# Strassen groups that accumulate on copies in PSUM: linear attention followed by a SiLU MLP

## The chip, the cores and the metric

The kernel runs on one core of one Trainium2 chip. The metric is the device time of one execution in microseconds (us). The engines are named as in the profile: PE is TensorE (matrix products), PEld its weight loads, DVE is VectorE, ACT is ScalarE, POOL is GpSimd, SP is SyncE (here it only issues DMAs). PSUM, where PE writes, has 8 banks of 128 partitions x 512 fp32 values.

## The reference

```python
# q, k, v: (batch 8, heads 8, seq 576, dim 64) fp32; w_in: 512 x 2048; w_out: 2048 x 512
q_s = exp(q - max(q, -1)); q_s = q_s / (sum(q_s, -1) + 1e-09)      # softmax over dim
k_s = exp(k - max(k, 2));  k_s = k_s / (sum(k_s, 2) + 1e-09)       # softmax over seq
kv = einsum('bhsd,bhse->bhde', k_s, v)
x = einsum('bhsd,bhde->bhse', q_s, kv)                             # (8, 8, 576, 64)
x = x.transpose(0, 2, 1, 3).reshape(4608, 512)
h = x @ w_in
out = (h * (1 / (1 + exp(-h)))) @ w_out                            # fp32, 4608 x 512
```

## The kernel before

All work runs in one pass over the 4608 tokens. The attention part goes batch by batch (576 tokens), the two products of the MLP chunk by chunk. Chunk 0 is the 576 tokens of batch 0, chunk 1 the 448 tokens up to token 1024, chunks 2 to 8 have 512 tokens each.

**Attention, batch b.** The loads `lq`, `lk`, `lv` come in two halves `c` of four heads each. ACT takes exp (`eq`, `ek`). DVE sums q's rows and inverts the sums (`z`). POOL scales q (`n`) and casts v to bf16 (`vc`). q is turned over by PE and copied out (`tr`, `tc`, batches 0 and 1) or by a DMA on SP's queue (`tq`). PE forms k^T v (`kv`), DVE scales it (`kc`). PE forms x^T (`X`), and ACT or DVE copies it to SBUF as fp16 (`x`). The trailing letter a or v of an operation says ACT or DVE. Batches 0 and 3 to 7 are loaded through SP's queue, batches 1 and 2 and all weights (`W1...`, `W2...`, converted to fp16 on the way) through POOL's.

**First product and SiLU.** Chunk 0 is done plainly, 16 blocks of 128 rows of h (`w`; tanh `h`; DVE `v`), and its second product too (`p`, in PSUM banks 2 to 5). Half of chunk 1 is plain (`m` in banks 0 to 3, with SiLU `mu`). The other half of chunk 1, and chunks 2 to 8 whole, use Strassen's algorithm in Winograd's form: per chunk two groups g (1 and then 0), each with seven half-size products P1 to P7 (`g{t}.{g}.{i}`, 8 matmuls of 256 columns each), with sums of weights `WS` made once and differences of x (`xs`) per chunk. Each product fills a pair of banks. P1, P6, P7 and P4 add up in banks 0 and 1. P2, P5 and P3 go to a second pair, which `other` names: 6 and 7 for group 1, 2 and 3 for group 0. The four output blocks are:

- U11 = P1 + P2
- U12 = P1 + P6 + P5 + P3
- U21 = P1 + P6 + P7 + P4
- U22 = P1 + P6 + P7 + P5

Before, bank 0's pair is copied to SBUF after P1, after P6 and after P7 (`s{t}.{g}.0`, `.1`, `.2`; `group_snap`, L398 to L400). DVE then adds the second pair to each copy (`a...`; `group_add`, L402 to L405), and ACT takes the SiLU of the three sums from SBUF and of bank 0 straight from PSUM (`u...`; `group_silu`, L407 to L409). The next product may go into a pair only when the copy or sum that reads it is done.

**Second product.** For chunks 1 to 8 it is Strassen as well: products `b{t}.{i}.{m}` (8 matmuls of 256 columns each, banks 4 and 5, L503), sums `S`, `T` and `sa`, `sb`, `sc`, `wa`, `wb`, `wc`, `wl`, and stores `o` on SP's queue. The last chunk's are named `e`, with stores spread over three queues (`q...`).

**Order.** The program issues operations by name from the string `ORDER`, from left to right; each goes to the end of its engine's queue, and an engine works its queue in that order. Waits between engines follow from the data. Before, chunk 0's start (loads, transposes, first x^T) is written out ahead of `ORDER`. The sums over SBUF operands on DVE are `S`, `T`, `WS` and `xs`.

Of the kernel before, what the change touches and what calls it, by code (L numbers as in the profile page):

```python
# [22 lines left out]
    vc1.1a vc1.1b gcopy WS1.3 kv1 lv2.1 tc1.1b p8 tc1.1a kc1 WS0.3 xt1.0 xt1.1 x1.0a x1.1v p9 x1.2a x1.3v  # L23
    g1.1.1 xs1.1 xs1.2 xs1.4 g1.1.2 s1.1.0a WS0.4 p10 xs1.3 eq2.0 a1.1.0 p11 eq2.1 z2.0 g1.1.6 g1.1.5
    s1.1.1a z2.1 n2.0 p12 ek2.0 g1.1.7 p13 s1.1.2v n2.1 ek2.1 p14 a1.1.2 g1.1.4 p15 tq2 u1.1.4 g1.1.3 po2v
    vc2.1 po1a m0 po3v po0a a1.1.1 u1.1.0 vc2.0 m1 lk3.0 mu0 m2 T2 lq3.0 mu1 lq3.1 m3 u1.1.2 lk3.1 T3 m4
    lv3.0 u1.1.1 lv3.1 m5 T4 mu2 os0 mu4 kv2 mu5 m6 mu3 kc2 X2.0 mu6 X2.1 x2.0v m7 x2.1a x2.3a x2.2v g2.1.1
    mu7 xs2.1 xs2.2 g2.1.2 s2.1.0v b1.1.0 ek3.0 S1.1 g2.1.6 eq3.1 lk4.0 S1.2 b1.2.0 os1 s2.1.1a b1.1.1 xs2.3
    xs2.4 eq3.0 a2.1.0 g2.1.7 vc3.0 sa1 b1.2.1 lq4.0 z3.1 s2.1.2a g2.1.5 vc3.1 ek3.1 b1.6.0 a2.1.2 n3.1
    lk4.1 g2.1.4 z3.0 g2.1.3 u2.1.0 g2.0.2 u2.1.4 wa1 n3.0 b1.6.1 a2.1.1 u2.1.2 g2.0.1 sb1 S1.3 kv3 tq3  # L30
    s2.0.0a b1.5.0 kc3 u2.1.1 S1.4 g2.0.6 b1.7.0 s2.0.1v lv4.0 ek4.1 b1.7.1 lv4.1 a2.0.0 os3 g2.0.7 sc1
    ek4.0 b1.5.1 s2.0.2v g2.0.5 eq4.0 lk5.0 wc1 lq4.1 g2.0.4 a2.0.2 os2 b1.4.0 vc4.0 lk5.1 z4.0 u2.0.4
    g2.0.3 u2.0.2 b1.3.0 lv5.0 vc4.1 a2.0.1 u2.0.0 lq5.0 b1.4.1 n4.0 X3.0 wl1v X3.1 kv4 x3.0a x3.1v x3.2a
    b1.3.1 kc4 x3.3a xs3.1 u2.0.1 g3.1.1 xs3.2 wb1 g3.1.2 s3.1.0a xs3.3 xs3.4 g3.0.2 S2.1 g3.1.6 S2.2 eq4.1
    b2.2.0 s3.1.1a b2.1.0 z4.1 ek5.0 b2.1.1 a3.1.0 g3.1.7 n4.1 sa2 ek5.1 b2.6.0 s3.1.2v g3.1.5 vc5.0 tq4
    g3.1.4 a3.1.2 u3.1.0 b2.6.1 u3.1.4 S2.3 g3.1.3 sb2 lq5.1 g3.0.1 u3.1.2 a3.1.1 lv5.1 lk6.0 b2.7.0 s3.0.0a
    o1.0 S2.4 b2.2.1 u3.1.1 a3.0.0 g3.0.6 lv6.0 b2.7.1 s3.0.1v eq5.0 g3.0.5 wa2 g3.0.7 sc2 lq6.0 z5.0 b2.4.0
    s3.0.2a lk6.1 b2.5.0 vc5.1 eq5.1 a3.0.2 g3.0.4 o1.1 n5.0 z5.1 g3.0.3 u3.0.4 b2.5.1 a3.0.1 n5.1 u3.0.0
    b2.4.1 wc2 u3.0.2 X4.0 X4.1 kv5 x4.1v x4.0a tq5 wl2v b2.3.0 u3.0.1 x4.3v g4.1.1 xs4.1 x4.2a b2.3.1 xs4.2
    s4.1.0a S3.1 g4.1.2 wb2 g4.1.6 lq6.1 a4.1.0 ek6.1 b3.1.0 xs4.3 s4.1.1a b3.1.1 xs4.4 S3.2 ek6.0 g4.1.5  # L40
    g4.1.7 sa3 eq6.0 b3.2.0 s4.1.2v eq6.1 b3.2.1 lq7.0 kc5 lk7.0 b3.6.0 a4.1.2 lv6.1 lq7.1 g4.1.4 o2.0 wa3
    g4.1.3 z6.0 u4.1.4 b3.5.0 u4.1.0 S3.3 g4.0.1 lk7.1 b3.6.1 a4.1.1 s4.0.0a g4.0.2 sb3 u4.1.1 g4.0.6 a4.0.0
    b3.5.1 s4.0.1a S3.4 b3.7.0 vc6.1 u4.1.2 g4.0.7 z6.1 vc6.0 g4.0.5 s4.0.2a b3.7.1 a4.0.2 n6.1 g4.0.4 sc3
    u4.0.2 g4.0.3 wc3 n6.0 b3.3.0 u4.0.4 a4.0.1 b3.4.0 u4.0.0 X5.0 X5.1 kv6 x5.0a x5.1v tq6 x5.3a x5.2v
    b3.3.1 u4.0.1 xs5.1 g5.1.1 xs5.2 wb3 b3.4.1 s5.1.0v o2.1 ek7.1 g5.1.2 kc6 g5.1.6 wl3a xs5.3 xs5.4 a5.1.0
# [25 lines left out]
def kernel(  # L71
# [9 lines left out]
    nc = tc.nc  # L81
# [196 lines left out]
    def xt_mm(b, cc, col, n, bank, dst):  # L278
        for r in range(2):
            for s in range(2):  # L280
                h = slice(s * 64, (s + 1) * 64)
                nc.tensor.matmul(  # L282
                    out=PS[r * 64:(r + 1) * 64, bank + s, dst:dst + n],
                    lhsT=kvn[b % 3][h, cc, r, :],
                    rhs=st[b]["qT"][h, col // P:(col + n) // P, cc, r * 64:(r + 1) * 64],
                )
# [7 lines left out]
    def x_mm(t, cc):  # L294
        for b, col, n, dst in pieces(t):
            xt_mm(b, cc, col, n, XBANK[2 * cc], dst)
# [114 lines left out]
    def group(t, g, i):  # L411
        bank = 0 if i in (1, 6, 7, 4) else other(t, g)
# [10 lines left out]
        for p in range(4):  # L423
            for c in range(2):
                nc.tensor.matmul(  # L425
                    out=PS[:, bank + p // 2, (p % 2) * HT:(p % 2) * HT + width(t)],
                    lhsT=a[:, c, p * 128:(p + 1) * 128],
                    rhs=bb[:, c, 0:width(t)],
                    start=(i in (1, 2, 5) and c == 0 and p % 2 == 0),
                    stop=(i in (2, 3, 4) and c == 1 and p % 2 == 1),  # L430
                    skip_group_check=True,
                )


# [404 lines left out]
```

## Time and profile before

| | |
|---|---|
| runs (3) | 257.86 us median, 256.9 to 258.57 |
| the profiled execution | 258.61 us |
| its span, first to last instruction | 256.6 us |
| PE, PEld busy | 249.1 us (97%), 204.2 us (80%) |
| DVE, ACT, POOL busy | 206.2 us (80%), 190.9 us (74%), 65.8 us (26%) |
| granted PE clock | 1.00 |
| HBM read, written | 36.70 MB, 9.44 MB |
| chain that ended last, largest parts | PE 76%, DMA 11%, issue 5% |

"Busy" is the time in which an engine has an instruction in work. The chain that ended last is followed back from the last instruction: at each step to what released it. A line with two names joined by `<-` reads output from input, with buffer numbers left out. In the groups by shape, the numbers behind the bar are the total busy time, the mean of one instruction in ns, and the engine's idle time just ahead of it with what ended that.

### The profile page before, as it was taken

The page shows a single profiled execution, that of the slowest core. Times are in us where ns is not written, and L with a number is a line of the kernel's source. Part 1 is how long each engine was busy: PE and PEld are TensorE (multiplying, and loading weights), DVE is VectorE, ACT ScalarE, POOL GpSimd, SP SyncE. Part 2 cuts the span into 40 slices and gives each one's busy share as a digit, 9 for nine tenths or more (in the row PEclk, how much of TensorE's full clock was granted, in tenths as well). Part 3 has the DMA queues.
Part 4 walks back from the last instruction along what each step waited for, and adds up shares of the span by engine and source line. Part 5 has one row for each costly group of instructions (what it writes and reads, how often), then busy time and mean ns, then how long its engine had stood idle before and what let it go on. Part 6 is the DMA issues. An engine that isn't in the chain of part 4 may idle for free.

```text
span 256.6 us, 6459 instructions
## 1 busy us (share of the span) xinstructions
PE 249.1 (97%) x2732; PEld 204.2 (80%) x2732; DVE 206.2 (80%) x276; ACT 190.9 (74%) x225; POOL 65.8 (26%) x62
## 2 busy tenths in 40 slices
PE   8799999999999999999999999999999999999994
PEld 3457746656888888888888888888888888888883
DVE  2958999888999898998987986896579836886752
ACT  5766876699999999999879988737587665664411
POOL 1753593650450622350073030006000000000022
PEclk9999999999999999999999999999999999999999
DMA  7999999979959957996874960021807000600365
GB/s 248 348 181 297 302 301 283 351 140 393 378 128 213 403 187 137 361 335 168 276 266 68 224 236 3 3 52 32 163 14 153 13 0 4 148 18 0 66 141 123
DMA packets 36044, 45.89 MB, mean 179 GB/s; under 512 B 16288, under 2 KB 21088, under 8 KB 36016
## 3 DMA queue, kind: packets, MB, share of 16 engines
q1 hardware_dynamic: 29456, 33.56, 45.5%
q0 software_dynamic: 6160, 11.60, 17.8%
q10 hardware_dynamic: 400, 0.33, 0.6%
q8 instruction: 21, 0.34, 0.5%
q14 instruction: 7, 0.06, 0.1%
HBM read 36.70 MB, written 9.44 MB: 180 GB/s over the span
## 4 chain that ended last, share of the span: by engine, by line
PE 76%; DMA 11%; issue 5%; POOL 3%; ACT 2%; DVE 1%; ACTq 0%; POOLq 0%
PE PS L503 37%; PE PS L425 33%; DMA qt<-in_q_dram 5%; DMA kt<-in_k_dram 5%; PE PS L335 3%; PE PS L248 2%; PE PS L282 2%; POOL W L564 1%; DMA out_dram<-ow 1%; POOL qt L152 1%; DVE GT L323 1%; ACT L409 0%; POOL W L570 0%; ACT sg L320 0%; ACT GT L409 0%
## 5 line engine op out<-in xcount | busy, mean ns | idle before, releaser
L403 DVE TENSOR_TENSOR h<-PS,h 128x1024 f32<-128x1024 f32 (+1 forms) x45 | 54.2, 1206 | 9.3 <-PE PS L425 7.8
L503 PEld LDWEIGHTS <-GT 128*128 128x128 f16 x512 | 50.1, 98 | 5.9
L425 PEld LDWEIGHTS <-WS 128*128 128x128 f16 x480 | 46.7, 98 | 6.5 <-issue 0.6
L409 ACT ACTIVATE GT<-h 128x1024 f16<-128x1024 f32 (+1 forms) x45 | 46.8, 1051 | 0.9 <-DVE h L403 0.7
L503 PE MATMUL PS<-W,GT 128*128 128x256 f16 x384 | 47.3, 273 | 0.0
L425 PE MATMUL PS<-XS,WS 128*128 128x256 f16 (+1 forms) x360 | 45.0, 272 | 0.0
L142 ACT COPY h<-PS 128x1024 f32<-128x1024 f32 (+1 forms) x31 | 31.1, 1003 | 16.9 <-PE PS L425 15.7
L503 PEld LDWEIGHTS <-S 128*128 128x128 f16 x384 | 37.1, 98 | 4.6
L425 PEld LDWEIGHTS <-W 128*128 128x128 f16 x360 | 35.2, 98 | 4.4
L216 POOL TENSOR_TENSOR eq<-eq,rzq 128x1152 bf16<-128x1152 bf16 x13 | 27.3, 2115 | 37.6 <-DVE rzq L211 36.3
L503 PE MATMUL PS<-T,S 128*128 128x256 f16 x256 | 32.2, 273 | 0.0
L144 POOL CAST vaug<-vt 128x1152 bf16<-128x1152 f32 x12 | 15.8, 1328 | 61.5 <-DMA vt<-in_v_dram 61.4
L425 PE MATMUL PS<-XT,W 128*128 128x256 f16 (+1 forms) x240 | 29.7, 272 | 0.0
L144 DVE COPY h<-PS 128x1024 f32<-128x1024 f32 (+1 forms) x14 | 17.0, 1212 | 9.2 <-PE PS L425 4.4
L207 DVE TENSOR_REDUCE zq<-eq 128x18 f32<-128x1152 bf16 x14 | 18.8, 1342 | 4.1 <-ACT eq L163 4.0
L163 ACT ACTIVATE eq<-qt 128x1152 bf16<-128x1152 f32 (+1 forms) x18 | 18.9, 1055 | 3.1 <-DMA qt<-in_q_dram 2.8
L168 ACT ACTIVATE ek<-kt 128x1152 bf16<-128x1152 f32 x16 | 18.6, 1163 | 3.0 <-DMA kt<-in_k_dram 2.9
L791 POOL DMA_DIRECT2D out_dram<-ow x5 | 2.7, 545 | 70.0 <-DVE ow L773 70.0
L409 ACT ACTIVATE GT<-PS 128x1024 f16<-128x1024 f32 (+1 forms) x15 | 15.2, 1013 | 6.1 <-PE PS L425 6.1
L503 PE MATMUL PS<-T,GT 128*128 128x256 f16 x128 | 16.3, 272 | 0.0
L307 PE MATMUL PS<-XT,W 128*128 128x288 f16 x128 | 16.0, 286 | 0.2 <-DMA W<-in_moe_w_in_dram 0.2
L503 PE MATMUL PS<-W,S 128*128 128x256 f16 x128 | 16.1, 273 | 0.0
(85 smaller groups left out, 332.4 us busy)
## 6 DMA issues: line engine op xcount, KB each, us to landing
out_dram<-ow SPq DMA_DIRECT2D x64, 128.0 KB, 3.0
qt<-in_q_dram SPq DMA_DIRECT2D x11, 576.0 KB, 5.9
kt<-in_k_dram SPq DMA_DIRECT2D x11, 576.0 KB, 7.5
vt<-in_v_dram SPq DMA_DIRECT2D x11, 576.0 KB, 6.6
qt<-in_q_dram POOLq DMA_DIRECT2D x4, 576.0 KB, 11.4
kt<-in_k_dram POOLq DMA_DIRECT2D x4, 576.0 KB, 13.9
vt<-in_v_dram POOLq DMA_DIRECT2D x4, 576.0 KB, 12.6
W<-in_moe_w_in_dram POOLq DMA_DIRECT2D x3, 512.0 KB, 10.6
```

Of the source, the lines that this page charges most:

```text
L142: eng.copy(out=o, in_=i)
L144: eng.tensor_copy(o, i)
L163: nc.scalar.activation(out=half(st[b]["eq"], cc)[:, :, g0:g1], in_=jgd(b, "qt", cc)[:, :, g0:g1], func=ACT.Exp)
L168: nc.scalar.activation(out=half(ek, cc), in_=jgd(b, "kt", cc), func=ACT.Exp)
L207: nc.vector.reduce_sum(out=z, in_=e, axis=AX.X)
L216: eng.tensor_tensor(out=e, in0=e, in1=r[:, :, :, None].to_broadcast([128, J, 2, D]), op=ALU.mult)
L307: nc.tensor.matmul(out=PS[:, WIDE[fb] + n, 0:S // 2], lhsT=W1[:, c, fb * 128:(fb + 1) * 128], rhs=XTS[0][:, c, n * (S // 2):(n + 1) * (S / ...
L335: nc.tensor.matmul(out=PS[:, bank, o0:TCH], lhsT=W1[:, c, fb * 128:(fb + 1) * 128], rhs=XTS[t % 2][:, c, o0:TCH], start=(c == 0), stop=(c ...
L403: nc.vector.tensor_tensor(out=four(t, i), in0=group_bank(t, g), in1=four(t, i), op=ALU.add)
L409: nc.scalar.activation(out=group_out(t, f, n), in_=x, func=ACT.Silu, scale=1.0 / XS)
L425: nc.tensor.matmul(out=PS[:, bank + p // 2, (p % 2) * HT:(p % 2) * HT + width(t)], lhsT=a[:, c, p * 128:(p + 1) * 128], rhs=bb[:, c, 0:wid ...
L503: nc.tensor.matmul(out=PS[:, bank, m * HN:(m + 1) * HN], lhsT=a[:, fc, m * 128:(m + 1) * 128], rhs=bb[:, fc, :], start=(first and fc == 0) ...
```

## The change

From chunk 2 on, a group works on copies in PSUM. After P1, bank 0's pair is copied into another pair, SB (`seed`, named `s{t}.{g}.1`): P2 is then added onto this copy by PE, and the pair holds U11. P5 goes to a third pair, SE, and is copied to SBUF (`snap5`, `s{t}.{g}.5`). After P6, DVE adds bank 0 and that SBUF copy and writes the sum back into SE (`add12`, `a{t}.{g}.12`); P3 is added onto it by PE, and SE holds U12. After P7, DVE adds bank 0 to the SBUF copy of P5 in place (`add22`, `a{t}.{g}.22`), which is U22. ACT takes the four SiLUs (`silu4`, `u{t}.{g}.11`, `.12`, `.21`, `.22`), three from PSUM and U22 from SBUF. SB is banks 2, 3 for group 0 and 6, 7 for group 1, SE the other way round. Chunk 1 keeps the copies and sums of before.

P2's matmuls start nothing new from chunk 2 on (`fresh`), and x^T's matmuls set their `start` flag only in the first of a chunk's pieces.

The start of chunk 0 is now in `ORDER` too, and the plain product of each 128-row block is cut into two halves, `w{fb}.0` (input rows 0 to 255) and `w{fb}.1`. `ORDER` is new from end to end up to `e1.0`; from there to the end it is as before. Sums of SBUF operands on DVE are placed where no POOL operation is planned, and what goes through SP's queue stays on it.

```diff
 ORDER = """
-    lk1.0 w1 lk1.1 w2 h1 w0 h2 v1 w3 h0 W2b1 w5 v0 v2 h3 w4 WS0.1 h5 w6 v3 h4 W2b2 v4 w7 v5 w8 h7 h6 v7 w9
-    lv1.0 h8 v6 w11 v8 h9 lv1.1 w10 eq1.0.0 v9 h11 WS0.2 w12 eq1.1.0 v11 h10 w13 WS1.1 eq1.0.1 v10 h12 w15
-    qp1a h13 v12 w14 eq1.1.1 v13 qp1b WS1.2 W2c1 p0 h14 z1.0 ek1.0 p1 z1.1.0 n1.0 z1.1.1 p2 h15 ek1.1 v15 p3
-    WS1.4 W2c2 tr1.0 v14 lq2.0 p4 tc1.0a tc1.0b lq2.1 n1.1 p5 W2d p6 lk2.0 T1 vc1.0 lk2.1 p7 tr1.1 lv2.0
...
-    mu7 xs2.1 xs2.2 g2.1.2 s2.1.0v b1.1.0 ek3.0 S1.1 g2.1.6 eq3.1 lk4.0 S1.2 b1.2.0 os1 s2.1.1a b1.1.1 xs2.3
...
+    ek0.0 tr0.0 heat1 n0.1 vc0.0 tc0.0a tc0.0b kv0.0 kc0.0 tr0.1 ek0.1 X0.0 heat2 vc0.1a vc0.1b tc0.1a tc0.1b kv0.1
+    kc0.1 heat3 x0.0a x0.0v X0.1 w0.0 x0.1a x0.1v w2.0 w3.0 w0.1 w2.1 w1.0 h0 w3.1 v0 w1.1 h2 v2 w4.0 h1 v1 w6.0
+    lv1.0 w6.1 w4.1 w5.0 w5.1 lk1.0 h3 h4 v3 w7.0 w7.1 h5 W2b1 h6 lv1.1 WS1.1 v4 v5 h7 w8.0 v6 w8.1 h8 w9.0 w9.1 h9
...
+    v10 eq1.1.0 WS0.1 h13 h12 w15.1 lq2.0 qp1b W2c1 v13 v12 h15 W2c2 w14.0 w14.1 p0 eq1.1.1 vc1.0 z1.0 n1.0 h14
+    z1.1.0 ek1.0 p1 p2 v15 p3 z1.1.1 lq2.1 vc1.1a v14 tr1.0 tc1.0a n1.1 vc1.1b lk2.1 ek1.1 p4 p5 tr1.1 tc1.0b tc1.1a
+    kv1 tc1.1b kc1 WS1.3 p6 xt1.0 x1.0a W2d xt1.1 p7 x1.1v g1.1.1 eq2.0 x1.2a s1.1.0a xs1.1 x1.3v WS1.4 xs1.2 p8
+    z2.0 g1.1.2 xs1.4 eq2.1 lk2.0 g1.1.6 p9 xs1.3 p10 a1.1.0 z2.1 s1.1.1a g1.1.5 g1.1.7 p11 s1.1.2v p12 p13 a1.1.2
+    lv2.1 lv2.0 n2.0 n2.1 g1.1.3 a1.1.1 g1.1.4 tq2 ek2.1 WS0.3 p14 lk3.0 vc2.1 gcopy ek2.0 u1.1.4 p15 T1 po2v po0a
+    po1a m0 T3 T2 m1 m3 u1.1.0 mu0 u1.1.1 lq3.0 vc2.0 m4 mu1 mu4 kv2 lq3.1 kc2 u1.1.2 po3v m5 m2 mu5 X2.1 x2.2v
+    lk3.1 mu3 X2.0 mu2 m7 x2.1a x2.0v xs2.1 x2.3a m6 mu7 g2.1.1 xs2.3 xs2.2 mu6 b1.1.0 ek3.0 lv3.0 lv3.1 S1.1 g2.1.5
+    s2.1.1v s2.1.5a b1.1.1 S1.2 g2.1.6 eq3.1 xs2.4 os0 sa1 b1.2.0 b1.2.1 a2.1.12 g2.1.7 lk4.0 eq3.0 g2.1.3 z3.1
+    g2.1.2 a2.1.22 g2.1.4 vc3.0 os1 ek3.1 z3.0 vc3.1 u2.1.11 u2.1.21 lq4.0 n3.1 b1.6.0 b1.6.1 g2.0.1 n3.0 S1.3
+    u2.1.22 kv3 lk4.1 sb1 tq3 b1.7.0 wa1 u2.1.12 T4 kc3 s2.0.1a WS0.2 lv4.0 b1.7.1 g2.0.2 lv4.1 WS0.4 vc4.0 sc1
...
     def group(t, g, i):
-        bank = 0 if i in (1, 6, 7, 4) else other(t, g)
+        if i in (1, 6, 7, 4):
+            bank = 0
+        elif t == 1:
+            bank = other(t, g)
+        else:
+            bank = SB[g] if i == 2 else SE[g]
+        fresh = (1, 2, 5) if t == 1 else (1, 5)
...
-                    start=(i in (1, 2, 5) and c == 0 and p % 2 == 0),
+                    start=(i in fresh and c == 0 and p % 2 == 0),
...
+    def pair(bank):
+        return PS[:, bank:bank + 2, :].rearrange("p b n -> p (b n)")
+
+    H5 = [None] * 2
+
+    def seed(g, eng):
+        copy(eng, pair(SB[g]), pair(0))
+
+    def snap5(g, eng):
+        H5[g] = mp.tile([128, 2 * TCH], FP32, name=f"h{g}", bufs=1)
+        copy(eng, H5[g], pair(SE[g]))
+
+    def add12(g):
+        nc.vector.tensor_tensor(out=pair(SE[g]), in0=pair(0), in1=H5[g], op=ALU.add)
+
+    def add22(g):
+        nc.vector.tensor_tensor(out=H5[g], in0=pair(0), in1=H5[g], op=ALU.add)
+
+    def silu4(t, g, x, f, n):
+        x = H5[g] if x is None else pair(x)
+        nc.scalar.activation(
+            out=group_out(t, f, n), in_=x.rearrange("p (f n) -> p f n", f=4), func=ACT.Silu, scale=1.0 / XS
+        )
+
+    SE = (6, 2)
+    SB = (2, 6)
...
+            both(f"s{n}1", seed, g)
+            both(f"s{n}5", snap5, g)
+            op(f"a{n}12", add12, g)
+            op(f"a{n}22", add22, g)
+            op(f"u{n}11", silu4, t, g, SB[g], 4 * g + 8, 0)
+            op(f"u{n}12", silu4, t, g, SE[g], 4 * g + 8, 1)
+            op(f"u{n}21", silu4, t, g, 0, 4 * g, 0)
+            op(f"u{n}22", silu4, t, g, None, 4 * g, 1)
```

More of the change, by code (lines that the diff above doesn't have):

```diff
@@ L29 @@
[L29 to L33, printed above, removed]
@@ L276, in pieces, with xt_mm @@
         return got
-    def xt_mm(b, cc, col, n, bank, dst):
+    def xt_mm(b, cc, col, n, bank, dst, start=True):
         for r in range(2):
@@ L285, in xt_mm @@
                     rhs=st[b]["qT"][h, col // P:(col + n) // P, cc, r * 64:(r + 1) * 64],
+                    start=start,
+                    stop=True,
+                    skip_group_check=True,
                 )
@@ L294, in x_mm @@
     def x_mm(t, cc):
[L295 to L296 removed]
+        for i, (b, col, n, dst) in enumerate(pieces(t)):
+            xt_mm(b, cc, col, n, XBANK[2 * cc], dst, i == 0)
     def x_out(t, c, eng):
@@ L641, in k_both @@
         kv(b, 1, bank)
+    for c in range(2):
+        for x, src in (("q", q), ("k", k), ("v", v)):
+            op(f"l{x}0.{c}", load, 0, x + "t", src, c, nc.sync)
+        op(f"eq0.{c}", exp_q, 0, c)
+        op(f"z0.{c}", qsum, 0, c)
+        op(f"n0.{c}", qnorm, 0, c, nc.vector)
+        op(f"ek0.{c}", exp_k, 0, c)
+        op(f"tr0.{c}", lambda c=c: (tr(0, c, 0, 5, 2 * c), tr(0, c, 5, J, 2 * c + 1)))
+        op(f"tc0.{c}a", trcopy, 0, c, 0, 5, 2 * c, nc.scalar)
+        op(f"tc0.{c}b", trcopy, 0, c, 5, J, 2 * c + 1)
+        op(f"kv0.{c}", kv, 0, c)
+        op(f"kc0.{c}", kvcopy, 0, c, c + 1)
+    op("vc0.0", vcast, 0, 0, nc.scalar)
+    op("vc0.1a", vcast, 0, 1, nc.scalar, 0, 1)
+    op("vc0.1b", vcast, 0, 1, nc.vector, 1, 2)
+    for c, b0, b1 in ((0, 4, 0), (1, 6, 2)):
+        op(f"X0.{c}", lambda c=c, b0=b0, b1=b1: (xt_mm(0, c, 0, 320, b0, 0), xt_mm(0, c, 320, 256, b1, 0)))
+        op(f"x0.{c}a", xt_evac, 0, c, b0, 0, 320, 0, nc.scalar)
+        op(f"x0.{c}v", xt_evac, 0, c, b1, 0, 256, 320, nc.vector)
+    for i, (n, bank) in enumerate(((20, 5), (7, 5), (3, 6), (2, 3))):
+        op(f"heat{i}", heat, n, bank)
+    op("gate", lambda: nc.gpsimd.tensor_copy(gate, st[0]["kt", 0][0:1, 1, 0:1]))
+    for x, f, n, c0, c1 in (("W1a0", 0, 4, 0, 2), ("W1a1", 0, 4, 2, 4), ("W1b", 4, 4, 0, 4), ("W1c", 8, 4, 0, 4), ("W1d", 12, 4, 0, 4)):
+        op(x, load_w1, f, f + n, c0, c1)
+    op("W2a", load_w2, 0, 4)
     for fb in range(NFB):
-        op(f"w{fb}", wide_mm, fb, range(2 if fb in (0, 2) else 0, NC))
+        op(f"w{fb}.0", wide_mm, fb, (0, 1))
+        op(f"w{fb}.1", wide_mm, fb, (2, 3))
         op(f"h{fb}", wide_tanh, fb)
```

137 lines of the change are left out of this document (41 added, 96 removed).

## Prediction

> **What bounds the kernel now.** I read five views, in this order. First the page's busy time by engine, then busy time by stretch, one stretch per token chunk:
>
> ```profile
> PE 249.1 (97%) x2732; PEld 204.2 (80%) x2732; DVE 206.2 (80%) x276; ACT 190.9 (74%) x225; POOL 65.8 (26%) x62
> ```
>
> ```profile
> 62.00:88.00 26.00, 26.00 (x380) 22.93 (x379) 24.92 (x33) 25.53 (x28) 10.81 (x7) 1.00 0.89 280
> 88.00:113.00 25.00, 25.00 (x305) 22.09 (x304) 23.21 (x29) 24.48 (x27) 8.88 (x6) 1.00 0.81 269
> 113.00:139.00 26.00, 26.00 (x316) 23.16 (x315) 21.84 (x30) 22.98 (x26) 7.24 (x4) 1.00 0.70 197
> ...
> 190.00:214.00 24.00, 24.00 (x224) 20.98 (x222) 17.08 (x20) 15.62 (x19) 0.00 (x0) 1.00 0.21 44
> ```
>
> The columns are stretch, length, then busy time of PE, PEld, DVE, ACT and POOL, then the granted clock (1.00), DMA share and GB/s. PE is busy for the whole of every stretch from 62 us on, while ACT falls from 98% of a chunk to 65% and DVE from 96% to 71%. The two slow engines can therefore be loaded to 98% without PE losing anything, and can be relieved without PE gaining anything.
>
> A busy PE is not a PE at its peak, so the third view is the chain of waits, for the pitch of the matmuls:
>
> ```profile
> 50.69 0.04 ACT ek L168
> 50.73 1.14 issue
> 51.87 1.28 ACT L409
> 53.16 0.93 ACT GT L409
> 54.09 0.04 issue
> 54.13 4.70 PE PS L335 x24
> ...
> 224.12 3.49 PE PS L425 x32
> ...
> 237.22 11.37 PE PS L503 x104
> ```
>
> Eight matmuls of 256 columns take 0.873 us, 109 ns each (3.49 us over 32). The 104 at the end, where DVE and ACT are mostly idle, have the same pitch (11.37 over 104). So the pitch is PE's own, and from 54.13 us on the chain lies on PE to 248.6. Ahead of 54.13 it is not PE that decides: the second k load of batch 2 lands at 50.6 (the DMA piece that ends there began at 38.30), then come exp (`ek2.1`, 1.16 us), a table load (1.28 us) and the SiLU `u1.1.4` (0.93 us), which frees bank 0 for the first matmul of `m0`. The fourth view, PE's waits, says how much that costs:
>
> ```profile
> PE PS L335 <- ACT GT L409: 0.6, 1, 0.6
> PE PS L445 <- DMA W<-in_moe_w_out_dram: 0.3, 1, 0.3
> PE PS L307 <- DMA W<-in_moe_w_in_dram: 0.2, 1, 0.2
> ```
>
> These are all of PE's waits between 15 us and 62 us; after 62 us the same view is empty. All that any reordering can win back from PE's waits is 1.1 us.
>
> The fifth view, the groups by shape, gives the prices:
>
> ```profile
> L403 DVE TENSOR_TENSOR h<-PS,h 128x1024 f32<-128x1024 f32 x42 | 50.9, 1214 | 9.3 <-PE PS L425 7.8 <-ACT h L142 1.1
> L409 ACT ACTIVATE GT<-h 128x1024 f16<-128x1024 f32 x42 | 44.1, 1056 | 0.9 <-DVE h L403 0.7
> L142 ACT COPY h<-PS 128x1024 f32<-128x1024 f32 x29 | 29.3, 1010 | 15.9 <-PE PS L425 14.8 <-ACT ow L536 0.4 <-ACT GT L409 0.3
> L144 DVE COPY h<-PS 128x1024 f32<-128x1024 f32 x13 | 15.9, 1222 | 8.5 <-PE PS L425 3.7 <-ACT GT L409 2.9 <-issue 1.8
> L487 DVE TENSOR_TENSOR W<-W 128x2048 f16<-128x2048 f16 x1 | 2.2, 2166 | 0.0
> ```
>
> **The change, part by part. Removed:** in chunks 2 to 8 there are 14 Strassen groups. Each had 3 copies, 3 sums and 4 SiLUs; each now has 2 copies (seed and P5), 2 sums and 4 SiLUs. That takes out 14 sums of 1.21 us (17 us of DVE) and 14 copies; by the diff's order ACT goes from 29 copies to 22, DVE from 13 to 6, so 7 x 1.01 = 7 us of ACT and 7 x 1.22 = 9 us of DVE. Of these 33 us nothing lies on the path: PE is full beside them. Matmuls are neither added nor taken away (7 products of 8 per group, as before). Part one: 0.
>
> **New operation: copies and sums that write PSUM.** No row of before shows DVE or ACT writing PSUM. The nearest rows read the same 128x1024 f32 from PSUM and write SBUF: 1.01 us on ACT, 1.21 to 1.22 on DVE. Lower bound: a 128x512 read, 0.59 and 0.69 us. Upper bound: reading and writing one after the other, two passes, 2.0 and 2.4 us. I take 1.01 and 1.22, as only the target differs.
>
> **New waits on PE.** Bank 0 holds P1; P6 may add to it only when the seed is copied, P7 only when `a..12` has read it, P4 only when `a..22` has, and the next group's P1 when `u..21` has. Before, copies stood at the same three places and the SiLU of bank 0 at the fourth. New are the waits of P2 on the seed and of P3 on `a..12`, whose result it adds to. Behind a waiting matmul everything on PE is queued, the products of the second matrix product too. In the new order two products (1.75 us) stand between P1 and P6 in most groups and two between P6 and P7, against a copy of 1.0 to 1.2 and some 0.1 us of semaphores: it fits where the engine is free. I walked ACT's and DVE's queues by these durations (0.1 less each when back to back, as starts in the trace show) through chunks 2 and 3, the densest. Chunk 2, group 0: with `g2.1.4` ending at 0, ACT runs `u2.1.11`, `u2.1.21` (to 1.9 with the table load ahead of them), `u2.1.22` 2.9, `sb1` 3.5, `u2.1.12` 4.5 and only then the seed, to 5.5; PE gets to `g2.0.2` after b1.6 (two), g2.0.1, kv3 and b1.7 (two), 5 x 0.87 + 0.7 = 5.05. Loss about 0.45 us. In chunk 3 the seed of group 1 stands behind a table load and an exp, loss 0.05; nothing else is late. From chunk 4 on ACT has more air by the stretches above. For chunks 4 and 5 I add 0.1. Part two: +0.6 us.
>
> **The start.** Its operations for chunk 0 are now named in the order, in the same sequence. The wide product is cut in two halves so that `w3.0` fills the 0.2 us in which `w1` waited for W1. On POOL's queue the v loads of batch 1 go ahead of the k loads, and `lk2.1` ahead of `W2d`: W2's last quarter comes one 576 KB load later. The last two k loads of before arrived 1.5 us apart (ACT's two exp start at 49.17 and 50.69), so `W2d` is 1.5 us later, at about 49.1 against 47.6; PE gets to `p12` with one product more behind it (0.77 us) and waits some 1.0 us there, 0.3 before. But `m0` still starts when the last k load is in: `lk2.0` now stands behind the same bytes as `lk2.1` did, followed by the same exp, table load and SiLU, so about 54.1 again, and PE, with 7 products of 0.77 to 0.86 left after `W2d`, needs until about 54.2. What is won or lost before goes into this wait: 0. After it, `b1.1.0` follows `mu6` with one group product less in between (0.87 us), but ACT had finished all of that stage by 62.4 and PE now gets there at 62.6: 0, at worst 0.9.
>
> **Sums beside GpSimd:** T3 took 2.17 us beside two casts, its like 1.21; moving such sums saves some 2 us of DVE, covered by PE. 0. The tail after `e1.0` is the same.
>
> **Sum:** the profiled execution has a span of 256.6 and took 258.61; +0.6 makes 257.2 and 259.2. It stands 0.75 above the median of the runs, 257.86, so against that median the forecast is 258.4 us.
>
> **The rivals.**
> 1. *Seeds queue behind ACT (slower).* In chunks 2 to 5 most seeds and P5 copies are on ACT, between exp, table loads and SiLUs, and P6 or P2 wait for them. For: ACT's 98% and 98% in the first two stretches; the walk finds 0.45 us in one group. Against: before had copies at the same places, at the same ACT load, and PE's waits are empty. Price: if each of those 8 groups loses that 0.45, 3.6 us, 261.5. It passes 1% (2.6 us) from 0.33 a group on. Chance 0.15.
> 2. *Writing PSUM costs two passes.* Then copy and sum take 2.4 on DVE and 2.0 on ACT against 1.75 us between products: with 0.15 of semaphores some 0.4 to 0.8 for each of about 18 tight places, 7 to 14 us, 265 to 272. Against: all PSUM readers cost 1.0 to 1.2 ns per column, with no sign of a second pass. Chance 0.05.
> 3. *The start comes forward.* If the early loads keep DMA fuller (283 GB/s and 351 GB/s in neighbouring slices) and the last k load lands one load's time earlier, the wait at `m0` goes and up to 1.5 us with it: 256.4, still within 1%. To pass 1% it would take 2.6, more than all PE's waits. Chance 0.08, of which 0.03 over 1%.
> 4. *PE isn't at its limit.* PE's gaps of 109 - 98 = 11 ns per matmul (a weight load takes 98 ns in the groups, and loads fill 80% of the span) would be waits for the engines that the change relieves; over the 1680 matmuls of 256 columns since 62 us that is at most 18 us, 240. Against: the same 109 ns where DVE and ACT idle. Chance 0.02. The Trainium skill, Perfetto Trace Analysis, section Identifying the Most-Contended Engine, speaks for this rival: matmul busy time is no measure of headroom and weight-load busy time is, by which a fifth would be to spare. The trace so far does not bear it out, by the pitch just named.
>
> **How the numbers follow.** The forecast has 0.70, the rivals 0.15, 0.05, 0.08 and 0.02. Its own range is 257.3 to 259.6. The range for 8 in 10 goes down to rival 3's 256.4 and up to rival 1's, 261.8. A measurement here tells about 1% from no change: faster by more 0.05 (rivals 3 and 4), slower by more 0.20 (rivals 1 and 2), the rest 0.75.
>
> **What would show it.** PE's waits after 62 us: a few tenths, with ACT's copy or DVE's sum as releaser, first before `g2.0.2`. PE busy in every stretch as now, ACT and DVE lower by some 10%. The copies into PSUM at 1.0 to 1.2 us. `m0` (L335's line) starting at 54.1 +- 0.5 with a longer wait for W2 ahead of it. It is wrong if PE waits over 2 us in all after 62 us, if a write to PSUM takes over 1.6 us, or if the matmul pitch is other than 109 ns.

## The result, and the profile after

The kernel after takes **258.97 us** (median of 20 runs, 257.57 to 260.43), the kernel before 257.51 us in 20 runs made with them: the ratio is 1.0053, with a 95% interval of 1.0038 to 1.0068. The change costs 0.5%, or 1.4 us (1.0 to 1.8). The profiled execution of after took 259.8 us, with a span of 258.0.

Busy time by engine, after:

```profile
PE 250.2 (97%) x2732; PEld 204.2 (79%) x2732; DVE 186.2 (72%) x255; ACT 183.4 (71%) x218; POOL 69.3 (27%) x62
```

PE has the same 2732 matmuls. DVE went from 206.2 to 186.2 us, ACT from 190.9 to 183.4. So 27.5 us of work went away on these two engines (POOL took 3.5 us more, 69.3 against 65.8), and the kernel is no faster. Busy time by stretch (length; PE, PEld, DVE, ACT, POOL; granted clock, DMA share, GB/s):

```profile
62.00:88.00 26.00, 25.84 (x378) 22.53 (x375) 23.68 (x27) 24.51 (x26) 11.28 (x7) 1.00 0.84 265
88.00:113.00 25.00, 24.75 (x304) 21.56 (x301) 20.93 (x27) 23.39 (x26) 10.07 (x7) 1.00 0.80 258
113.00:139.00 26.00, 26.00 (x316) 23.14 (x315) 18.95 (x26) 24.79 (x28) 6.53 (x5) 1.00 0.70 191
139.00:165.00 26.00, 24.89 (x305) 21.89 (x304) 18.97 (x25) 19.36 (x22) 8.89 (x4) 1.00 0.49 130
```

The last of these stretches before:

```profile
139.00:165.00 26.00, 26.00 (x317) 23.12 (x315) 22.13 (x29) 23.73 (x26) 2.26 (x2) 1.00 0.50 131
```

PE, full in every stretch before, lacks 0.16, 0.25 and 1.1 us here, and the largest hole is not in the densest stretch but at 139 to 165, where ACT is down to 74%. PE's waits after 62 us (engine, line, what it waited for; total, times, longest), a view that was empty before:

```profile
PE PS L433 <- ACT GT L463: 1.1, 1, 1.1
PE PS L538 <- DVE S L512: 0.2, 1, 0.2
PE PS L433 <- DVE PS L456: 0.2, 1, 0.2
```

This view counts a wait from the modelled end of the matmul ahead. The starts of the matmuls tell a little more: a matmul of 256 columns starts 109 ns after the one ahead if nothing holds it. What the starts after 62 us lose against that adds up to **2.5 us** here (1.27 at 151.01, 0.33 at 67.43, 0.33 and 0.25 at 97.06 and 98.19, 0.17 at 227.99, and crumbs) and to 0.3 us in the kernel before. I call this "lost starts" from here on.

The chain that ended last, around the largest of them:

```profile
135.84 2.13 POOL eq L215
137.98 6.38 DMA qT<-eq
...
145.50 1.15 ACT ek L167
...
147.72 1.28 ACT L463
149.02 1.95 ACT GT L463 x2
150.97 0.04 issue
151.01 1.03 PE PS L433 x8
...
238.63 11.37 PE PS L538 x104
```

Read upward from 151.01: the first product of chunk 5's second group (`g5.0.1`, into bank 0) waits for the second of two SiLUs (`u5.1.21`, which reads bank 0), these for a table load, that for exps, and the first exp for the transposing DMA of q, which POOL fed 6.4 us earlier. The last line has the pitch: 11.37 us over 104 matmuls, 109 ns, as before. The new forms, in the groups by shape:

```profile
L456 DVE TENSOR_TENSOR PS<-PS,h 128x1024 f32<-128x1024 f32 x14 | 17.2, 1232 | 20.3 <-ACT h L141 11.2 <-PE PS L433 9.1
L141 ACT COPY PS<-PS 128x1024 f32<-128x1024 f32 x11 | 11.0, 1003 | 3.7 <-PE PS L433 1.9 <-DVE XT L143 0.9 <-ACT XT L141 0.7
```

A sum written to PSUM takes 1232 ns (1214 into SBUF), a copy 1003 ns (1010 into SBUF).

### The profile page after: what moved, and what is told of

Same layout as the page of the kernel before. It is cut to its first block, busy times and chain, and to the rows that moved or that the text cites. A ratio compares the mean times of both kernels' runs of the same rounds, so it can differ in the third digit from the quotient of the medians.

```text
span 258.0 us, 6444 instructions
## 1 busy us (share of the span) xinstructions
PE 250.2 (97%) x2732; PEld 204.2 (79%) x2732; DVE 186.2 (72%) x255; ACT 183.4 (71%) x218; POOL 69.3 (27%) x62
## 4 chain that ended last, share of the span: by engine, by line
PE 68%; DMA 14%; DVE 6%; issue 5%; ACT 3%; POOL 2%; ACTq 0%; DVEq 0%; POOLq 0%
PE PS L538 30%; PE PS L433 30%; DMA W<-in_moe_w_in_dram 6%; DMA kt<-in_k_dram 5%; PE PS L480 3%; DMA qT<-eq 2%; PE PS L337 2%; DVE S L512 2%; PE PS L247 2%; PE PS L281 1%; DVE PS L456 1%; DVE h L459 1%; ACT ek L167 1%; POOL eq L215 1%; DMA out_dram<-ow 1%
## 5 line engine op out<-in xcount | busy, mean ns | idle before, releaser
L463 ACT ACTIVATE GT<-PS 128x1024 f16<-128x1024 f32 x42 | 42.1, 1024 | 16.8 <-PE PS L433 16.7
L215 POOL TENSOR_TENSOR eq<-eq,rzq 128x1152 bf16<-128x1152 bf16 x13 | 29.5, 2269 | 31.2 <-DVE rzq L210 27.7
L433 PE MATMUL PS<-XT,W 128*128 128x256 f16 (+1 forms) x240 | 30.9, 272 | 1.1 <-ACT GT L463 1.1
L456 DVE TENSOR_TENSOR PS<-PS,h 128x1024 f32<-128x1024 f32 x14 | 17.2, 1232 | 20.3 <-ACT h L141 11.2
L143 POOL CAST vaug<-vt 128x1152 bf16<-128x1152 f32 x12 | 16.9, 1408 | 42.2 <-DMA vt<-in_v_dram 42.2
L459 DVE TENSOR_TENSOR h<-PS,h 128x1024 f32<-128x1024 f32 x14 | 17.0, 1214 | 5.7 <-PE PS L433 5.6
L143 DVE CAST XT<-PS 128x512 f16<-128x512 f32 (+1 forms) x17 | 11.2, 679 | 6.9 <-PE PS L281 6.9
L141 ACT COPY h<-PS 128x1024 f32<-128x1024 f32 (+1 forms) x13 | 12.9, 994 | 4.5 <-PE PS L433 4.3
## 6 DMA issues: line engine op xcount, KB each, us to landing
vt<-in_v_dram POOLq DMA_DIRECT2D x4, 576.0 KB, 12.3
```

Of the source, the lines that this page charges most:

```text
L141: eng.copy(out=o, in_=i)
L143: eng.tensor_copy(o, i)
L215: eng.tensor_tensor(out=e, in0=e, in1=r[:, :, :, None].to_broadcast([128, J, 2, D]), op=ALU.mult)
L433: nc.tensor.matmul(out=PS[:, bank + p // 2, (p % 2) * HT:(p % 2) * HT + width(t)], lhsT=a[:, c, p * 128:(p + 1) * 128], rhs=bb[:, c, 0:wid ...
L456: nc.vector.tensor_tensor(out=pair(SE[g]), in0=pair(0), in1=H5[g], op=ALU.add)
L459: nc.vector.tensor_tensor(out=H5[g], in0=pair(0), in1=H5[g], op=ALU.add)
```

## The experiments

All times are medians, with the ratio to the kernel before as run beside it. Four theories stood at the start: **Q**, the wait behind ACT's queue at `g5.0.1`; **P**, the groups on copies in PSUM cost a little everywhere; **S**, the start; **G**, sums slowed beside GpSimd.

**The kernel after, unaltered, and the kernel before, unaltered.**

> The changed kernel unaltered, as the measure for the others. Its ratio to the kernel before should again be 1.005. If PE's stalls are made by the order of the queues, they stand again at the same products: about 1.3 us ahead of the first product of chunk 5's group 0 (g5.0.1), 0.3 ahead of g2.1.7, 0.3 and 0.25 near b2.6.1 and g3.1.4. If they are chance (DMA landing times), they move or change by more than 0.5 us, and so does the 0.85 us wait for W1 at 19.7 us.

Measured: 259.01 us, 1.0063 (1.0048 to 1.0078). Lost starts after 62 us 2.1 us, 1.25 of them at 150.2 in front of `g5.0.1` again. That stall is no accident of one execution, and neither are the two at 97 us (0.33 and 0.25, here at 96.29 and 97.42). The 0.33 at 67.43 did not come again: there `S1.2` took 1.22 us, while in the first profile it met a cast and took 1.85. Nor did the 0.7 us that PE waited for W1 ahead of 62 us in the first profile of after.

> The kernel before, unaltered, for a second profile. The first stood 1.1 us above the median of its 20 runs and had 1.9 us of stalls on PE between 15 and 62 us. If these are chance of that execution (DMA landing late), this profile shows less than 0.8 us of them, a span of about 255.3 and the ratio 1.000; if they belong to the kernel's queue order, the 0.76 us at m0 and the 0.46 us at p12 stand here again, and the changed kernel's start is worth 0.8 us or more.

Measured: 257.19 us, 0.9981 (0.996 to 1.0002), the spread of this comparison. Its profile is of an execution of 257.12 us with a span of 255.1, and PE's waits from 15 us on are **empty**, `m0` starting at 52.64. The 1.1 us that the first profile of before showed ahead of 62 us, the wait at `m0` among them, did not come again. From the start of `m0` to the start of the last matmul PE takes 198.5 us in both profiles of before, 200.7 and 200.2 in the two of after. The differences, 2.2 and 1.7 us, are the growth of the lost starts (2.1 and 1.7): behind `m0` nothing else of note was lost.

**Is it the exp on ACT's queue? (Q)** ACT in before (start, length, line, form, and in brackets the idle time ahead of it):

```profile
144.16 1.16 ACT L163 ACTIVATE eq<-qt 128x1152 bf16<-128x1152 f32 x1 [0.19 <-DMA qT<-eq]
145.24 1.15 ACT L168 ACTIVATE ek<-kt 128x1152 bf16<-128x1152 f32 x1
146.40 1.28 ACT L409 ACT_TABLE_LOAD   x1
```

and in after:

```profile
144.44 1.16 ACT L162 ACTIVATE eq<-qt 128x1152 bf16<-128x1152 f32 x1 [1.30 <-DMA qT<-eq]
145.50 1.15 ACT L167 ACTIVATE ek<-kt 128x1152 bf16<-128x1152 f32 x1
146.56 1.15 ACT L162 ACTIVATE eq<-qt 128x1152 bf16<-128x1152 f32 x1
147.72 1.28 ACT L463 ACT_TABLE_LOAD   x1
149.02 1.94 ACT L463 ACTIVATE GT<-PS 128x1024 f16<-128x1024 f32 x2
```

In both, `eq7.1` writes the one buffer that the transposition of batch 6 must have read first. Before, the transposition landed at 144.1 and ACT lost 0.19 us. After, ACT was at that point 0.8 us sooner (143.1 against 144.0), the transposition 0.3 later, and the new order put a third exp (`eq7.0`) ahead of the table load and the SiLUs. Two runs part the two: one moves that exp, the other gives the exps of q a second buffer.

```diff
 e1: ORDER
-... g5.1.4 eq7.0 ...   ... g5.0.5 z7.0 ...
+... s5.0.5a eq7.0 ...  ... a5.0.12 z7.0 ...
 e2
-    st[b]["eq"] = ap.tile([128, J, NG * D], BF16, name="eq")
+    st[b]["eq"] = ap.tile([128, J, NG * D], BF16, name="eq", bufs=2)
```

(In e2 the buffer of the tanh, `sg`, is taken from those named `ow`, to make room.)

> The exp eq7.0 is moved on ACT from ahead of the SiLU u5.1.21 to behind the copy s5.0.5a, and its row sum z7.0 on DVE behind a5.0.12; nothing else. Theory Q (ACT's queue): g5.0.1 waits for u5.1.21, which stands behind three exp, the first of which waits for the transpose of q; one exp of 1.06 us less in front leaves about 0.2 us of the 1.27 us wait, so 1.0 us less, ratio to before about 1.001. Theory P (the new waits on copies in PSUM cost a little everywhere): no more than 0.2 us. Theory S (the start): 0.

Measured: 259.81 us, 1.0111 (1.0084 to 1.0139), slower than after. The stall at `g5.0.1` fell from 1.25 to 0.28 us, and a new one of 2.2 us stands at 159.8. PE's waits and ACT's queue ahead of it:

```profile
PE PS L537 <- ACT sc L553: 2.0, 1, 2.0
```

```profile
154.46 1.28 ACT L161 ACT_TABLE_LOAD   x1
155.76 1.17 ACT L161 ACTIVATE eq<-qt 128x1152 bf16<-128x1152 f32 x1
156.94 1.28 ACT L462 ACT_TABLE_LOAD   x1
158.23 1.02 ACT L462 ACTIVATE GT<-PS 128x1024 f16<-128x1024 f32 x1
```

The stall went as theory Q expected, the total did not: an exp standing alone among SiLUs costs 1.2 us and two table loads of 1.28.

> The tile eq gets two buffers, so that eq7.1 need not wait until the transpose of batch 6 has read the one buffer (to make room, the tanh results of chunk 0 use the tile of the output, three buffers as before). Theory Q: the 1.30 us in which ACT idles until 144.4 us go, and with them the 1.27 us wait at g5.0.1: ratio about 1.000. If instead the exp themselves are too many there, whatever they wait for, most of the wait stays. Theories P and S: 0.

Measured: 258.05 us, 1.0035 (1.002 to 1.005). No stall is left at 150 us, and lost starts after 62 us are 0.8 us. ACT in e2, where the three exps still stand ahead of the table load:

```profile
141.85 1.17 ACT L162 ACTIVATE eq<-qt 128x1152 bf16<-128x1152 f32 x1
...
146.43 1.94 ACT L464 ACTIVATE GT<-PS 128x1024 f16<-128x1024 f32 x2
```

The first exp now waits for nothing. By the ratios the second buffer wins back 0.28% of the 0.63%, 0.7 us (1.0 by the medians), less than the whole that was expected. **Q holds** for this stall, and it takes both causes: without the wait for the transposition (e2) it is gone, and with one exp fewer in front (e1) most of it is.

**Sums beside GpSimd (G).** DVE in after, and POOL at the same time:

```profile
93.61 1.23 DVE L456 TENSOR_TENSOR PS<-PS,h 128x1024 f32<-128x1024 f32 x1
94.75 2.25 DVE L512 TENSOR_TENSOR S<-S,GT 128x2048 f16<-128x2048 f16 x1
96.93 1.21 DVE L459 TENSOR_TENSOR h<-PS,h 128x1024 f32<-128x1024 f32 x1
```

```profile
93.81 2.12 POOL L215 TENSOR_TENSOR eq<-eq,rzq 128x1152 bf16<-128x1152 bf16 x1 [5.30 <-DVE rzq L210]
95.87 2.15 POOL L143 CAST vaug<-vt 128x1152 bf16<-128x1152 f32 x1
```

`S2.2` takes 2.25 us where an S sum alone takes 1.22, and it is stretched by about the time for which POOL's scaling still runs. The sum with one operand in PSUM beside the same instruction keeps its 1.23. POOL pays in turn: the cast at 95.87, which begins while `S2.2` still runs, takes 2.15 us where one alone takes 1.16, and the scaling at 71.78, begun inside the sum of 71.55, takes 2.90 where one alone takes 2.12. In each of these meetings the one that began second is longer, by about what was left of the first. Four S sums of after (at 64.05, 94.75, 131.20 and 152.26) are stretched by 3.2 us together (in e0 two, by 2.0); in before it was one, by 0.5. The plan holds in the order, but POOL and DVE meet elsewhere: POOL's casts of v start when their load lands, not where they stand in the list. Three runs move such sums:

```diff
 e3: ORDER
-... z4.1 ... a3.1.12 S2.2 ...        ... S1.2 ... a2.1.12 ...
+... S2.2 ... a3.1.12 z4.1 ...        ... a2.1.12 S1.2 ...
 e6: e2, and in ORDER
-... z4.1 ... a3.1.12 S2.2 ...        ... S2.4 ... S2.3 ...
+... S2.2 ... a3.1.12 z4.1 ...        ... S2.3 S2.4 ...
 e7: e6, and in ORDER
+... a3.0.12 S2.4 ...  a2.1.12 S1.2 ...  a2.1.22 z3.1 ...
```

> On DVE, S2.2 goes ahead of z4.1 (2.25 us beside GpSimd at 94.8 us, its like take 1.22), z4.1 behind a3.1.12, and S1.2 behind a2.1.12 (1.85 us beside a cast). Theory G (sums slowed beside GpSimd delay the sum or product that PE waits for): the stalls of 0.32 at g2.1.7 and 0.33 and 0.25 at b2.6.1 and g3.1.4 go, 0.6 to 0.9 us, ratio about 1.002; the one at g5.0.1 stays at 1.2. Theory Q alone: no change over 0.2 us in the total. Theory P: the stalls stay where they are, as they come with the copies and not with the sums.

Measured: 260.28 us, 1.0117 (1.0096 to 1.0137), slower and not faster as G had it. At the place aimed at it did what G says: `S2.2` ran alone at 93.17 in 1.23 us, and the two stalls at 97 us are gone. But two others came (PE's waits):

```profile
PE PS L432 <- DVE h L458: 1.4, 1, 1.4
PE PS L432 <- ACT GT L462: 1.1, 1, 1.1
PE PS L537 <- DVE GT L511: 0.6, 1, 0.6
```

The first, at 71.2, is the sum `a2.1.22`, now standing behind `S1.2` (still beside a cast, 1.75 us) and a `z`. The third, at 102.9, is `S2.3`, now beside the scaling and cast that `S2.2` had met, 2.16 us behind an `S2.4` of 2.35.

> The changed kernel with two buffers for eq, S2.2 ahead of z4.1, z4.1 behind a3.1.12 and S2.3 ahead of S2.4 (S1.2 stays where it was). If the two causes named so far (ACT waiting for the transpose with three exp behind it; sums slowed beside GpSimd) are the whole loss, PE's stalls after 62 us are 0.2 us in all and the ratio to before is 1.000 (0.998 to 1.002). If the slowed sums only hand the stall on, 0.5 us or more stands near 103 us as in the run with the sums moved, ratio 1.003. If copies in PSUM cost anything beyond these waits (theory P), the ratio stays above 1.003 with PE free of stalls.

Measured: 258.2 us, 1.0027 (1.0003 to 1.0051). The lost starts after 62 us stay at 0.85; the slowed sums are now `S2.3` and `S2.4` (2.35 and 2.17 us), and `b2`'s product waits behind them at 102.7. That is the case of the expectation in which the slowed sums only hand the stall on. Against e2 (1.0035) nothing that can be told apart.

> The changed kernel with two buffers for eq and every sum that ran beside GpSimd in chunks 2 and 3 put where nothing on PE waits for it or for what follows it: S1.2 behind a2.1.12, z3.1 behind a2.1.22, S2.2 ahead of z4.1, z4.1 behind a3.1.12, S2.3 ahead of S2.4, S2.4 behind a3.0.12. If the transpose and the slowed sums are the whole loss after 62 us, PE's stalls there are at most 0.3 us in all (0.3 in the kernel before) and the ratio to before is 0.999 to 1.002; what stays is the start. If copies in PSUM cost something beyond PE's waits (theory P), the ratio stays at 1.003 or above with PE free of stalls after 62 us. If the stall is handed on again, 0.4 us or more stands at a new place.

Measured: 259.87 us, 1.0087 (1.0055 to 1.0118). The stall was handed on once more. `T4` is slowed beside the scalings of batch 3 in after too (2.54 us, here 2.53), but here it began at 74.67 instead of 73.22, behind an `S1.3` of 1.92 us, and `kc3`, behind it, came late. PE's waits:

```profile
PE PS L433 <- DVE kvn L259: 0.9, 1, 0.9
PE PS L538 <- DVE GT L512: 0.8, 2, 0.4
PE PS L538 <- DVE ow L558: 0.7, 1, 0.7
```

So G is true of each sum, but three orders made by it won nothing: in each, POOL's work in chunks 2 and 3 met some other sum. That no order can keep them apart is not shown; the order of before has one such meeting of an S sum there (1.75 us at 74.23).

**The start (S).** The order of before up to the first group, then that of after:

```diff
 e5: ORDER
-    ... w4.0 h1 v1 w6.0 lv1.0 w6.1 w4.1 w5.0 w5.1 lk1.0 ... mu7 g2.1.1 ...
+    ... w2.0 lk1.0 w1.0 w1.1 lk1.1 w2.1 h1 w0.1 h2 v1 ... mu7 xs2.1 g2.1.1 ...
```

> The changed kernel with the start (all up to the first group of chunk 2) in the order of the kernel before; mu7 and xs2.1 stand at the seam, what the start already does is left out of the rest. If the start is a gain of the change (theory S), this is 0.8 us or more slower than the changed kernel, ratio to before about 1.009. If the start is worth nothing either way, the ratio stays at 1.005 to 1.006 and PE's stalls after 62 us are the same, 1.25 at g5.0.1 and 0.6 near 97 us.

Measured: 259.41 us, 1.0071 (1.0045 to 1.0097), not to be told from after (the intervals leave some 0.8 us open). `m0` starts between 52.64 and 54.13 us in the four profiles with the old order of the start (both of before, e5, and e11 below) and between 52.65 and 53.62 in the ten with the new one. As far as these runs can tell, the start is worth nothing either way, and S is out.

**Is PE's length the whole of it?** The prediction put all engine work but PE's at nothing; theory L below says the same of this part. Four runs in chunks 6 to 8, where DVE and ACT of after are busy for 52 to 64% of a stretch and POOL is idle until the tail. First less PE work:

```diff
 e8: group
+        if i == 3 and t >= 6:
+            return
```

> The kernel after, with the product P3 left out of the six groups of chunks 6 to 8 (48 of 2732 matmuls of 256 columns; U12 lacks it). Theory L (TensorE's own pitch of 109 ns is the limit there): 48 x 0.109 = 5.2 us less, about 253.8 us against the 259.0 of the kernel after, ratio to the kernel before 0.986; VectorE and ScalarE, at 52 to 64% of these stretches, follow at once. Rival 4 of the prediction (the gaps of TensorE are waits for VectorE and ScalarE): their work is the same, so clearly less than half of that is won, 256.4 or more.

Measured: 255.55 us, 0.9925 (0.99 to 0.9951), that is 3.5 us below after (1.0063 x 257.48 = 259.1) and not 5.2. PE's waits have a new line:

```profile
PE PS L435 <- DVE h L461: 1.4, 3, 0.6
```

Three times P4 now waits for the sum `a..22`, by 0.61, 0.53 and 0.76 us at the starts, 1.9 together; 5.2 - 1.9 = 3.3. P3 had been the cover of that sum. The pitch is the limit, as theory L says, and the difference is lost cover. Rival 4's side, 256.4 or more, is not met.

Then more work for the others:

```diff
 e9: add22, t >= 6: behind the sum, for both halves of H5[g]
+                nc.vector.tensor_tensor(out=more, in0=half, in1=half, op=ALU.add)
+                nc.scalar.activation(out=more, in_=more, func=ACT.Copy, scale=1.0)
 e10: the same behind U22's SiLU, the copy from the half itself
+                nc.vector.tensor_tensor(out=more[0], in0=half, in1=half, op=ALU.add)
+                nc.scalar.activation(out=more[1], in_=half, func=ACT.Copy, scale=1.0)
 e11: e10's lines in the kernel before, behind the SiLU of its sum 2
```

> The kernel after, with work added in the six groups of chunks 6 to 8 that nothing needs: behind the second sum, two sums of 128x512 on VectorE from SBUF to SBUF (about 0.6 us each) and a copy of each in place on ScalarE (about 0.5 us each), some 7 us more of VectorE and 6 us more of ScalarE, about what the change took out there. Theory L: TensorE has no room to lose or win; the time stays at the 259.0 of the kernel after within 0.3 us, ratio 1.006, and TensorE waits at most a few tenths longer, where a needed sum stands behind an added one. Rival 4: what the change took out of these engines counts, so 3 us or more are lost, 262 or more.

Measured: 265.48 us, 1.0304 (1.0278 to 1.033), 6.4 us above after, the time that rival 4 named (262 or more). ACT's waits from 160 us on give another reason:

```profile
ACT sg L465 <- DVE sg L464: 15.0, 6, 4.5
```

ACT stood 15 us in six waits at the added copies, with SiLUs that PE needed queued behind them. So this run prices the placing of the copies as much as their length. The next one has no such wait.

> As the run before with added work, but the added work waits for nothing that comes late: both added sums (128x512, SBUF to SBUF, about 0.6 us each, on VectorE) and both added copies (128x512, SBUF to SBUF, about 0.5 us each, on ScalarE) read the finished U22 and are issued right behind its SiLU, six times, in chunks 6 to 8: again some 8 us more of VectorE and 6 us more of ScalarE. Theory L (only TensorE's length counts; what the run before lost, it lost because the added copies on ScalarE stood waiting for a late VectorE sum, with needed SiLUs behind them): 259.0 as the kernel after, at most 0.6 more, TensorE's waits as there. Rival: the work itself counts, because VectorE and ScalarE were short of room there after all: 263 or more again, with TensorE waiting at the same places.

Measured: 263.07 us, 1.0244 (1.0219 to 1.027), still 4.4 us above after (1.0063 x 257.02 = 258.6). Theory L's "at most 0.6" is refuted, and the time is the one that its rival named. Busy time in two of the stretches, then ACT at one of the new stalls:

```profile
190.00:214.00 24.00, 23.73 (x218) 20.42 (x217) 16.86 (x21) 11.79 (x16) 0.00 (x0) 1.00 0.21 45
214.00:240.00 26.00, 24.82 (x224) 21.70 (x222) 17.19 (x22) 15.34 (x22) 0.00 (x0) 1.00 0.19 42
```

```profile
172.50 1.05 ACT L463 ACTIVATE GT<-h 128x1024 f16<-128x1024 f32 x1
173.45 1.28 ACT L470 ACTIVATE sg<-h 128x512 f32<-128x512 f32 x2
174.64 1.92 ACT L463 ACTIVATE GT<-PS 128x1024 f16<-128x1024 f32 x2
```

DVE and ACT are at 49 to 70%, so their whole time does not run short as the rival had it, and yet PE loses starts, seven times by 0.3 to 0.8 us. The added pair of copies (1.28 us) stands ahead of the SiLU that frees bank 0, and the next group's first product starts at 175.69 with 0.82 us lost.

> The kernel before, with the same added work as the run before (two sums of 128x512 on VectorE and two copies of 128x512 on ScalarE behind the SiLU of U22, in each of the six groups of chunks 6 to 8), which cost the kernel after some 4 us. Theory T (the groups on copies in PSUM have less slack than the old ones: each of their products hangs on a copy or sum that ended just before): the old groups take the added work nearly without loss, under 1.5 us, ratio under 1.006. Rival (any order made for given durations loses when an engine's queue grows by 1.3 us at a spot, in the old groups as in the new, whatever the busy share): 3 us or more here too, ratio 1.012 or more, and TensorE waits where a SiLU or copy that frees bank 0 stands behind an added copy.

Measured: 259.49 us, 1.0079 (1.0052 to 1.0107), 2.0 us for the added work (15.7 us on the two engines, 8.2 and 7.5, in this kernel as in e10). By lost starts it cost 2.0 us in the old groups and 3.7 in the new (5.8 against the 2.1 of the unaltered run). Neither side of the expectation was met: the old groups pay too, and about half as much. That fits theory T, that the new groups have less slack, but the added operations stand at other neighbours in the two orders, so it is not shown by this alone.

## Why the prediction was right, and where it was not

**The end and its side: right, the closeness in part by luck.** 258.4 was forecast and 258.97 measured, inside the likeliest case's own range. No difference over 1%, and slower by some tenths of a percent, because PE's length sets the end and the change takes none of it away. But as a change it was +0.6 us forecast and 1.4 measured. The forecast was counted from 257.86, while the kernel before came out at 257.51 in the runs beside it, which brought the two ends closer. And the waits that make the kernel slower are not those from which the 0.6 was added up, as the term on new waits below shows.

**Part one, 33 us of DVE and ACT work for nothing: right.** ACT fell by 7.5 us as forecast. On DVE 26 us were forecast and 20.0 came: sums and copies fell by 25.2, and 3.5 us came back as S and T sums beside POOL. (The remaining 1.8 us is a matter of counting: neighbouring instructions overlap by about 0.1 us, which busy time counts once, 14.1 us in all before and 12.3 after.)

**Copies and sums into PSUM: right.** 1.01 and 1.22 us were taken, 1003 and 1232 ns measured. Rival 2, two passes, is out. So is P as a price on every group: in after one product alone waited for a seed, by 0.17 us (at 227.99), and behind `m0` the lost starts are the whole loss.

**New waits on PE: the mis-sized term.** +0.6 us was forecast; lost starts grew by 2.1 us in the first profile of after and by 1.7 in the second (2.5 and 2.1 against 0.3). By the view of the waits they stay under the 2 us that was named as the bound (1.5), by the starts they pass it. The 0.45 us at `g2.0.2` did not come:

```profile
70.25 1.98 ACT L463 ACTIVATE GT<-PS 128x1024 f16<-128x1024 f32 x2 [0.18 <-PE PS L433]
...
74.60 1.00 ACT L141 COPY PS<-PS 128x1024 f32<-128x1024 f32 x1
```

```profile
76.21 1.04 PE L433 MATMUL PS<-XT,W 128*128 128x256 f16 x8
```

That product started at 76.21, 5.05 us after `g2.1.4` ended (71.16), just as the walk had it; but the seed was done at 75.60, 4.4 us after that end and not the walk's 5.5. The walk had hung `u2.1.11` on P4, while it hangs on P2 and began at 70.25, with the table load done ahead of it. The waits that did come are two: 1.27 us at `g5.0.1`, in the chunks for which 0.1 had been added on the ground that ACT has more air, and 0.9 us behind slowed sums at 67 and 97 us. The first needed a walk of ACT's queue through chunk 5 with the DMA that its exp waits for, and not the busy share; e2 shows it: with the second buffer that stall is gone. The second kind is borne out too: with `S2.2` moved, the two at 97 us are gone (e3), and the one at 67 us is missing where `S1.2` met no cast (e0).

**Sums beside GpSimd: wrong sign.** They were priced as 2 us of DVE saved and put at 0, on the word of the order that such sums lie apart. The stretched S sums went from 0.5 to 3.2 us, and PE waited for them. The Trainium skill, SBUF — State Buffer, section Who interferes with whom, says that a VectorE instruction with two SBUF inputs contends with a GpSimd instruction that reads SBUF, that one with at most one SBUF input, outside its 2-port modes, does not, and that the order of issue decides which of the two blocks. The trace agrees: 1.22 to 2.25 us for the one, 1.23 unchanged for the other, and 1.16 to 2.15 for the cast that began second.

**The start: the sum was right, its reasons were not.** Forecast 0; e5 finds no difference. But the chain ahead of 54.13, the wait at `m0` and rival 3's price of up to 1.5 us were read from an execution 0.75 us above the median. In b0's profile none of those waits is there, and `m0` starts at 52.64; e11, which has the same start, shows none either. After has it at 53.37, below the 53.6 that was named as the lower end, and without a wait; nor did the 1.0 us forecast at `p12` come. In executions like b0's there was no such 1.5 us to win.

**"Can be loaded to 98% without PE losing anything": wrong.** The other half of that sentence, that PE gains nothing if they are relieved, is what the result shows. But e10 loses 4.4 us with these engines at 49 to 70%. The share of a stretch that was full by a fitting order does not say that other work fits.

**The rivals.** Rival 1 had the right kind of thing, a release that stands behind ACT's queue, at the wrong operation (seeds) and at eight places where one came. That the range went up to 261.8 is not worked out in the prediction: rival 1's own price is 261.5. Rival 4 (gaps of PE are waits for the others) is refuted by e8, and by the pitch of 109 ns, which in after is the same at 62 to 88 us (DVE busy for 91%, ACT for 94%) and at 190 to 214 (64% and 52%). The reading that the prediction set against it was half wrong: at the end of before, from 237.2 to 248.6, ACT is mostly idle (3.41 us busy), but DVE is busy for 8.03 of the 11.4 us. The Trainium skill, Perfetto Trace Analysis, section Identifying the Most-Contended Engine, would have PE's room judged by the busy share of weight loads (and by arithmetic done against the peak) and not by that of matmuls. Here weight loads were 79% of the span in after while the matmuls stood at their 109 ns with nothing to spare, and the measurement decides.

**What stays open.** With the second buffer the kernel is still slower by 0.9 us (0.5 to 1.3), of which lost starts after 62 us account for 0.5; from `m0` to the last matmul PE takes 199.0 us there against 198.5. The rest lies ahead of `m0`, where executions scatter by more than that, or in the scatter of the runs, and stays open. What an order without any sum beside POOL would give was not measured. How little slack the new groups have against the old was not settled by a run that puts both into one order.

## What to carry to other kernels

Where the bound engine was full, relieving the others won nothing, and a new order that is otherwise neutral is judged by the waits that it opens. Price those by walking each in-order queue with everything its instructions wait for, DMAs and single buffers too, in every stretch; the busy share says neither that added work fits (at 49 to 70% it cost 4 us) nor where a wait comes. A small wait in one profile should be looked for in a second execution before a price is built on it.

## What else the runs showed

- Writing PSUM from DVE or ACT cost what writing SBUF did, as the prediction took it: 1232 against 1214 ns and 1003 against 1010 ns for 128x1024 fp32.
- An fp16 sum of two SBUF operands, 128x2048, takes 1.22 us alone and 1.4 to 2.35 us, once 3.13 (e7), where it begins beside POOL's scaling or casting (the T sums up to 2.54). POOL's instruction keeps its time if it began first (2.12 us for a scaling) and is stretched if it began second (2.90 us). Where a sum was moved away, the next one took its place.
- A matmul of 256 columns keeps its 109 ns in every kernel here, whether ACT is busy for 98 or for 49% of a stretch; only the starts behind a late copy, sum or SiLU move.
